# Extra bfloat16 products on TensorE ahead of the first expert, and one exponential moved on ScalarE

## Chip, core and metric

The kernel runs on one core of one Trainium2 chip. The metric is the device time of one execution in microseconds (us). The engines are PE (TensorE; PEld is its loading of weights), DVE (VectorE), ACT (ScalarE), POOL (GpSimd) and SP (SyncE, which only issues transfers).

## What is computed

Two halves share the input `x = A_q` (2048 tokens of 512 channels) and are mixed by a gate per token:

```
g = sigmoid((x * gate_w).sum(-1))
a = q * (causal_conv(shift_conv(k) * v, ssm_k) + D * ...)      # long convolution by FFT
b = sum over the top 2 of 8 experts: gate_e * (silu(x Wg) * (x Wu)) Wd
out = g * a + (1 - g) * b
```

The expert of a token is chosen by the two largest of its eight router logits `x @ w_router`. Each expert has 1376 hidden units. Everything is float32; the kernel splits the factors of its large products into a high and a low part of PE's faster 32-bit type and multiplies three times.

## The kernel before

One core does all of it. PE is the busy engine. The order of a run is this:

1. **Router.** SP loads the transposed input in 16 pieces `xt` (4 batches `c` of 4 pieces of 256 KB). For each batch PE multiplies the four pieces by the router weights, each into 32 partitions of one bank `lgp` (L509), ACT copies the bank to `lgT` (`keep`, L472), and PE turns it into `lg_ps` (`turn`, L488), nine columns for each of 16 token blocks; column 8 is the gate's logit. DVE copies the logits and ranks them (`ranks`, L493). `turn(c-1)` and `ranks(c-1)` are written between the two halves of batch `c`; those of the last batch come after the loop (L511).
2. **Counts and the first list.** DVE makes a mask and a running count (L518, L520), PE sums it over partitions into `cn_ps` (L526, L527), DVE works out the place of each token of the fullest expert and a table `hots` of ones and zeros (L535 to L618), PE turns the table into a list of token numbers (L624), DVE writes it as `gidx` (L600).
3. **First gather.** POOL fetches the listed rows by five indirect transfers (`load_rows`, L372); PE transposes each block of 128 rows (`turn_rows`, L381), ACT and DVE write its two parts `xh` and `xl` (L383, L384).
4. **Experts.** For each of 8 experts and 11 groups of hidden units PE does gate and up products `g` and `u` (`up`, L755, by `mm3`, L186), and down products (L804). The long convolution runs as filler between them (`tick`, L349).

Between the steps 1 to 3 stand pieces of the convolution's first stage on its kernel `ssm_k`: `plan(k)` (L461) issues `k_out` for the pieces named in `SEQ`: PE multiplies `kr` by `c` into two banks (`ks..p`, L239), ACT evicts each (L221) and issues its write to `kd` (L222). `plan(0)` issues piece `ks1`, `plan(2)` `ks2` and `ks3`, `plan(4)` `ks4` and `ks5`.

Up to L638 the order on all engines is the order in which the code is written (`tc.manual_schedule`, L432, closed at L638); after it a scheduler in the framework orders the instructions by its own timeline. PE, ACT, DVE and POOL each work through their queue in order. PSUM has eight banks; `lg_ps`, `lgp`, `cn_ps` and the experts' `g` and `u` share three of them (tag `gu`). `sums` (L439) is a bfloat16 tile whose parts 2 and 3 POOL fills with 1.0 and -1.0 at the very start (L440, L441).

The exponential of the gate's logits, `G` (L522), reads `lg_ps` on ACT; before the change it is written after `plan(0)`, so behind both evictions of `ks1`.

Of the kernel before, what the change touches and what calls it, by code (L numbers as in the profile page):

```python
# [14 lines left out]
AF = mybir.ActivationFunctionType  # L15
# [7 lines left out]
D = 512  # L23
KT = D // P
F = 1376
E = 8
PL = S // P
# [26 lines left out]
XG = 3  # L54
Z0, Z1 = (7, 6)
RM = 5
SEQ = "o0||o1 o2||o3 o4".split("|")
SEQ_N = max(int(w[1:]) for w in " ".join(SEQ).split() if w[0] == "o") + 1
VD = (1, 2, 3, 4, 5, 6)
# [70 lines left out]
def gated_mix(ctx: ExitStack, tc: tile.TileContext, a, out):  # L130
    nc = tc.nc
    sync, act, dve, pool, pe = nc.sync, nc.scalar, nc.vector, nc.gpsimd, nc.tensor
# [14 lines left out]
    G = cp.tile([P, PL], F32, name="G")  # L147
# [19 lines left out]
    def turned(name):  # L167
        return ps.tile([P, D], F32, tag="y", bufs=3, name=name)
# [84 lines left out]
    def k_load(pl):  # L253
        kr[pl] = load("B", BB, f"kr{pl}", rows(a["ssk"], pl), late=KL)
        if pl == 0:
            dD = t2k("T", 3, "dD")[0:1, :]
            sync.dma_start(dD, a["ssd"])
            pool.tensor_add(kr[0][0:1, :], kr[0][0:1, :], dD)

    def k_out(pl):  # L260
        stage1_f32(kr[pl], kd, pl, f"ks{pl}")
# [172 lines left out]
    lg_ps = ps.tile([P, D], F32, tag="gu", bufs=3, name="lg_ps")  # L434
# [4 lines left out]
    sums = rp.tile([P, 4, P], BF16, name="sums")  # L439
# [21 lines left out]
    def plan(k):  # L461
        for w in SEQ[k].split():
            i = int(w[1:])
            if w[0] == "l":
                k_load(k_order[i])
            else:
                k_out(k_order[i])
# [4 lines left out]
    def keep(c):  # L472
        lgT.append(rp.tile([P, D], F32, tag="lgT", bufs=4, name=f"lgT{c}"))
        act.activation(lgT[c], lgp[c], AF.Copy)
# [7 lines left out]
    lgv = lg_ps[:, :PL * 16].rearrange("p (a b) -> p a b", b=16)  # L482
# [5 lines left out]
    def turn(c):  # L488
        for pl in range(c * CP, c * CP + CP):
            pe.matmul(lg_ps[:, pl * 16:pl * 16 + E + 1], lgT[c][:, pl % CP * P:pl % CP * P + P], pick, start=True, stop=True)  # L490


    def ranks(c):  # L493
        part = slice(c * CP, c * CP + CP)
        dve.tensor_copy(L[:, part], lgv[:, part, :E])
        for x in range(E):
            for lo, hi, cmp in ((0, x, ALU.is_ge), (x + 1, E, ALU.is_gt)):
                if hi > lo:
                    dve.tensor_tensor(gt[:, part, lo:hi, x], L[:, part, x:x + 1].to_broadcast([P, CP, hi - lo]),
                                      L[:, part, lo:hi], op=cmp)  # L500
        dve.tensor_reduce(rank[:, part], gt[:, part], op=ALU.add, axis=AX.X)

    for c in range(NB):
        lgp.append(ps.tile([P, D], F32, tag="gu", bufs=3, name=f"lgp{c}"))
        for kt in range(KT):
            if c and kt == 2:
                turn(c - 1)
                ranks(c - 1)
            pe.matmul(lgp[c][32 * kt:32 * kt + 32], wk[:, kt], xts[c * KT + kt], start=True, stop=True)  # L509
        keep(c)  # L510
    turn(NB - 1)  # L511
    ranks(NB - 1)
    pool.tensor_copy(sums[:, 0], before)
    pool.tensor_add(before, before, ident)
# [4 lines left out]

    dve.tensor_tensor_scan(run[:, 1:].rearrange("p e a -> p (e a)"), ones, mask.rearrange("p e a -> p (e a)"),  # L520
                           0.0, op0=ALU.mult, op1=ALU.add)
    act.activation(G, lgv[:, :, E], AF.Exp, scale=-1.0)  # L522
    plan(1)
    cn_ps = ps.tile([P, D], F32, tag="gu", bufs=3, name="cn_ps")
    for o, (x, y) in ((0, (2, 3)), (16, (0, 1))):
        pe.matmul(cn_ps[:, o:o + E], sums[:, x], run[:, 1:, PL - 1], start=True, stop=False)  # L526
        pe.matmul(cn_ps[:, o:o + E], sums[:, y], run[:, :E, PL - 1], start=False, stop=True)  # L527
    plan(2)
    cnt = cn_ps[:, :E]
    key = rp.tile([P, E], F32, name="key")  # L530
    top = rp.tile([P, 1], F32, name="top")
# [60 lines left out]
    def read(k, pv):  # L592
        c0, n, f0, f1 = chunks[k]
        cs = slice(c0, c0 + n)
        m = min(MAIN, c0 + n)
        if f0 == 0:
            dve.tensor_scalar(idf[:, cs], pv[:, 0], dummy, None, op0=ALU.add)
            dve.tensor_add(idf[:, cs], idf[:, cs], pv[:, 1])
            if c0 < MAIN:
                i = dve.tensor_scalar(gidx[:, c0:m], idf[:, c0:m], float(S - 1), None, op0=ALU.min)  # L600
                anchor.setdefault("dve", i.ins)
                anchor.setdefault("dve k", i.ins)
        if f1 > 2:
            dve.scalar_tensor_tensor(wsum[:, cs], idf[:, cs], float(S), spare[:, cs], op0=ALU.is_ge, op1=ALU.mult)
            dve.tensor_add(sidx[:, cs], idf[:, cs], wsum[:, cs])
            dve.tensor_copy(wsum[:, cs], pv[:, 2 - f0])
            dve.tensor_add(wsum[:, cs], wsum[:, cs], pv[:, 3 - f0])
            dve.tensor_add(slot_w[:, cs], wsum[:, cs], pv[:, 4 - f0])
# [12 lines left out]
    list0 = ps.tile([P, D], F32, tag="y", bufs=3, name="list0")  # L621
    pv0 = list0[:, :2 * TILES].rearrange("p (f c) -> p f c", f=2)
    for i in range(PL):
        pe.matmul(pv0, hot[:, i], val0[:, i], start=(i == 0), stop=(i == PL - 1))  # L624
    read(0, pv0)
    l1, z, ll = mi2[:, 224:240], mi2[:, 240:256], te(mf2, PL * E)
# [6 lines left out]
    rows0 = gather(0)  # L633
    next(rows0)
    plan(4)
    for _ in range(RM):
        next(rows0, None)
    order.close()  # L638
    ordered = False
    for _ in rows0:  # L640
# [285 lines left out]
    with tc.For_i(0, nb_v, 1) as b:  # L926
        with tc.tile_pool(name="over", bufs=1) as op:
# [9 lines left out]
            p = turned("oxp").rearrange("p (k n) -> p k n", k=KT)  # L937
# [5 lines left out]
            for ft, (f0, fw) in enumerate(FT):  # L943
                n = 2 * KT * fw
# [66 lines left out]
```

## Time and profile before

| | us |
|---|---|
| three runs | 985.08, 985.34, 989.24; median 985.34 |
| the profiled execution | 989.02 |
| its span, first to last instruction | 987.2 |
| mean granted PE clock in it | 0.981 of full speed |
| PE busy | 956.7 (97%) |
| DVE, ACT, POOL busy | 658.1, 559.3, 163.2 |

Busy time is the sum of an engine's instruction times, overlaps counted once. The granted clock stands at one of two levels, 2.4 GHz (1.00) and 1.2 GHz (0.50). All times below count from the start of the span.

### The profile page before, as it was taken

The page shows a single profiled execution, that of the slowest core. Times are in us where ns is not written, and L with a number is a line of the kernel's source. Part 1 is how long each engine was busy: PE and PEld are TensorE (multiplying, and loading weights), DVE is VectorE, ACT ScalarE, POOL GpSimd, SP SyncE. Part 2 cuts the span into 40 slices and gives each one's busy share as a digit, 9 for nine tenths or more (in the row PEclk, how much of TensorE's full clock was granted, in tenths as well). Part 3 has the DMA queues.
Part 4 walks back from the last instruction along what each step waited for, and adds up shares of the span by engine and source line. Part 5 has one row for each costly group of instructions (what it writes and reads, how often), then busy time and mean ns, then how long its engine had stood idle before and what let it go on. Part 6 is the DMA issues. An engine that isn't in the chain of part 4 may idle for free. (4 is left out here: it accounts for less than half of the span.)

```text
span 987.2 us, 18708 instructions
## 1 busy us (share of the span) xinstructions
PE 956.7 (97%) x6944; PEld 876.0 (89%) x6944; DVE 658.1 (67%) x1318; ACT 559.3 (57%) x1066; POOL 163.2 (17%) x165
## 2 busy tenths in 40 slices
PE   7699999999999999999999999999999999999995
PEld 3388998999999999999999999999999999867893
DVE  3599569979999754756766576675776567554541
ACT  1464334554555643787677777688776777513330
POOL 0202010210203020131111312041113010023202
PEclk7699999999999999999999999999999999999998
DMA  7775694455656544576545646475557552699813
GB/s 253 266 263 192 238 312 153 151 169 180 213 191 181 179 134 167 152 181 185 160 140 161 167 150 198 147 171 157 180 154 190 158 175 84 206 305 273 213 31 43
DMA packets 88400, 178.24 MB, mean 181 GB/s; under 512 B 10513, under 2 KB 19601, under 8 KB 88178
## 3 DMA queue, kind: packets, MB, share of 16 engines
q1 hardware_dynamic: 54322, 119.40, 37.1%
q0 software_dynamic: 19296, 30.08, 15.3%
q10 hardware_dynamic: 14688, 27.53, 7.5%
q8 instruction: 56, 0.92, 0.4%
q14 instruction: 38, 0.31, 0.1%
HBM read 133.39 MB, written 43.57 MB: 179 GB/s over the span
## 5 line engine op out<-in xcount | busy, mean ns | idle before, releaser
L187 PE MATMUL g<-xh,gh 128*128 128x256 f32 (+13 forms) x704 | 203.7, 289 | 0.0
L187 PE MATMUL u<-xh,gh 128*128 128x256 f32 (+13 forms) x704 | 201.8, 287 | 1.7 <-ACT sg L786 1.6
L188 PE MATMUL u<-xl,gh 128*128 128x256 f32 (+13 forms) x704 | 201.1, 286 | 0.0
L189 PE MATMUL g<-xh,gl 128*128 128x256 f32 (+13 forms) x704 | 201.0, 286 | 0.0
L189 PE MATMUL u<-xh,gl 128*128 128x256 f32 (+13 forms) x704 | 200.9, 285 | 0.0
L188 PE MATMUL g<-xl,gh 128*128 128x256 f32 (+13 forms) x704 | 200.9, 285 | 0.0
L187 PEld LDWEIGHTS g<-xh,gh 128*128 128x128 f32 (+1 forms) x704 | 131.0, 186 | 14.9 <-issue 5.4
L187 PEld LDWEIGHTS u<-xh,gh 128*128 128x128 f32 (+1 forms) x704 | 131.1, 186 | 6.3 <-issue 2.3
L188 PEld LDWEIGHTS g<-xl,gh 128*128 128x128 f32 (+1 forms) x704 | 131.1, 186 | 3.8 <-issue 0.8
L189 PEld LDWEIGHTS u<-xh,gl 128*128 128x128 f32 (+1 forms) x704 | 131.0, 186 | 3.0 <-issue 1.6
L189 PEld LDWEIGHTS g<-xh,gl 128*128 128x128 f32 (+1 forms) x704 | 131.1, 186 | 2.5 <-issue 0.8
L188 PEld LDWEIGHTS u<-xl,gh 128*128 128x128 f32 (+1 forms) x704 | 131.1, 186 | 1.8
L788 ACT ACTIVATE hh<-sg 128x256 fp32r<-128x256 f32 (+13 forms) x176 | 73.7, 419 | 98.1 <-DVE sg L787 96.6
L187 PE MATMUL yp<-hh,dh 128*128 128x266 f32 (+10 forms) x440 | 127.4, 290 | 0.0
L188 PE MATMUL yp<-hl,dh 128*128 128x266 f32 (+10 forms) x440 | 126.8, 289 | 0.0
L189 PE MATMUL yp<-hh,dl 128*128 128x266 f32 (+10 forms) x440 | 126.6, 289 | 0.0
L787 DVE TENSOR_TENSOR sg<-sg,u 128x256 f32<-128x256 f32 (+13 forms) x176 | 74.8, 425 | 75.9 <-PE u L189 55.3
L771 DVE TENSOR_TENSOR gl<-raw,gh 128x1024 fp32r<-128x1024 f32 (+1 forms) x88 | 105.3, 1197 | 24.7 <-ACT gh L769 24.2
L786 ACT ACTIVATE sg<-g 128x256 f32<-128x256 f32 (+13 forms) x176 | 67.5, 386 | 80.0 <-PE g L189 73.2
L769 ACT ACTIVATE gh<-raw 128x1024 fp32r<-128x1024 f32 (+1 forms) x88 | 91.2, 1036 | 34.0 <-PE u L188 29.7
L789 DVE TENSOR_TENSOR hl<-sg,hh 128x256 fp32r<-128x256 f32 (+13 forms) x176 | 75.3, 428 | 32.7 <-ACT hh L788 32.2
L801 DVE TENSOR_TENSOR dl<-rd,dh 128x512 fp32r<-128x512 f32 (+1 forms) x88 | 59.5, 687 | 52.3 <-ACT dh L799 48.0
(1035 smaller groups left out, 1801.0 us busy)
## 6 DMA issues: line engine op xcount, KB each, us to landing
raw<-in_wgu SPq DMA_DIRECT2D x77, 512.0 KB
rd<-in_wd SPq DMA_DIRECT2D x77, 256.0 KB
kl<-kd SPq DMA_DIRECT2D x32, 256.0 KB
xl<-xd SPq DMA_DIRECT2D x32, 256.0 KB
zd<-ze ACTq DMA_DIRECT2D x32, 256.0 KB
zl<-zd SPq DMA_DIRECT2D x32, 256.0 KB
out<-zt SPq DMA_DIRECT2D x21, 256.0 KB
krow<-in_kpad SPq DMA_DIRECT2D x19, 256.0 KB
```

Of the source, the lines that this page charges most:

```text
L187: pe.matmul(p, wh, hi, start=start, stop=False)
L188: pe.matmul(p, wh, lo, start=False, stop=False)
L189: pe.matmul(p, wl, hi, start=False, stop=stop)
L769: act.activation(gh[:, :n], raw[:, :n], AF.Copy)
L771: dve.tensor_sub(gl[:, :n], raw[:, :n], gh[:, :n].bitcast(F32))
L786: act.activation(sg[:fw, :nn], pp[0][:fw, :nn], AF.Silu)
L787: dve.tensor_mul(sg[:fw, :nn], sg[:fw, :nn], pp[1][:fw, :nn])
L788: act.activation(hh[:fw, sl], sg[:fw, :nn], AF.Copy)
L789: dve.tensor_sub(hl[:fw, sl], sg[:fw, :nn], hh[:fw, sl].bitcast(F32))
L801: dve.tensor_sub(dl[:fw], rd[:fw], dh[:fw].bitcast(F32))
```

## The change

A helper `warm(n, p)` issues `n` products of a 128x128 tile of ones by a 128x256 tile of ones and minus ones, both bfloat16, into columns 256 to 511 of the bank `p`. Nobody reads these columns. `WARM` gives the counts: 14 before the router, 2 after each of the four products of batch 0 (8 in all), 6 before the last `turn`, 16 before the counts, 20 before the list, 6 in its middle, 26 before the first transposes, and 8 after each of the first four blocks of transposes (32): 128 products in all. The exponential `G` moves from behind `plan(0)` to just behind the last `turn`.

```diff
+WARM = (14, 2, 6, 16, 20, 6, 26, 8)
...
+    def warm(n, p):
+        for _ in range(n):
+            pe.matmul(p[:, D // 2:], sums[:, 2], sums[:, 2:].rearrange("p a b -> p (a b)"), start=True, stop=True)
+
+    warm(WARM[0], lg_ps)
     for c in range(NB):
...
             pe.matmul(lgp[c][32 * kt:32 * kt + 32], wk[:, kt], xts[c * KT + kt], start=True, stop=True)
+            if c == 0:
+                warm(WARM[1], lg_ps)
         keep(c)
+    warm(WARM[2], lg_ps)
     turn(NB - 1)
+    act.activation(G, lgv[:, :, E], AF.Exp, scale=-1.0)
     ranks(NB - 1)
...
-    act.activation(G, lgv[:, :, E], AF.Exp, scale=-1.0)
     plan(1)
+    warm(WARM[3], lg_ps)
     cn_ps = ps.tile([P, D], F32, tag="gu", bufs=3, name="cn_ps")
...
     plan(2)
+    warm(WARM[4], cn_ps)
...
     for i in range(PL):
+        if i == PL // 2:
+            warm(WARM[5], cn_ps)
         pe.matmul(pv0, hot[:, i], val0[:, i], start=(i == 0), stop=(i == PL - 1))
...
     plan(4)
-    for _ in range(RM):
+    warm(WARM[6], cn_ps)
+    for i in range(RM):
         next(rows0, None)
+        if i < RM - 1:
+            warm(WARM[7], cn_ps)
     order.close()
```

How the instructions stand now is shown at three places. The line numbers after the change are some 1 to 17 higher.

**DVE's copy of the last batch of logits**, with the semaphores that each instruction waits for. Before:

```order
L501 TENSOR_REDUCE r_160<-gt 128x32 [waits DVE_49]
L495 COPY r_160<-lg_ps 128x32 [waits PE_49]
L499 TENSOR_TENSOR gt<-r_160 128x4x7 [waits DVE_49]
```

After:

```order
L502 TENSOR_REDUCE r_160<-gt 128x32 [waits DVE_49]
L496 COPY r_160<-lg_ps 128x32 [waits Activation_49]
L500 TENSOR_TENSOR gt<-r_160 128x4x7 [waits DVE_49]
```

The copy waited for PE's `turn`; now it waits for ACT, that is for the exponential that reads the same bank.

**ACT from the exponential to the first weights' high part** (`gh`), `s` being a small tile of the routing. Before:

```order
L221 ACTIVATE ks1e_284<-ks1p_278 128x512
L222 DMA kd<-ks1e_284 128x512 [waits DMAHW7_49,Activation_49]
L522 ACTIVATE G<-lg_ps 128x16 [waits DVE_49]
L750 TENSOR_LOAD eor_78 [waits DVE_49]
L221 ACTIVATE ks2e_300<-ks2p_296 128x512 [waits PE_49]
L222 DMA kd<-ks2e_300 128x512 [waits DMAHW2_49,Activation_49]
L221 ACTIVATE ks2e_303<-ks2p_297 128x512
L769 ACTIVATE gh_0_469<-raw_0_467 128x1024 [waits DMAHW0_49]
L222 DMA kd<-ks2e_303 128x512 [waits DMAHW3_49,Activation_49]
L221 ACTIVATE ks3e_310<-ks3p_306 128x512 [waits DMAHW6_49,PE_49]
```

After:

```order
L222 ACTIVATE ks2e_347<-ks2p_341 128x512
L223 DMA kd<-ks2e_347 128x512 [waits DMAHW2_49,Activation_49]
L222 ACTIVATE ks3e_354<-ks3p_350 128x512 [waits DMAHW6_49,PE_49]
L223 DMA kd<-ks3e_354 128x512 [waits DMAHW3_49,Activation_49]
L222 ACTIVATE ks3e_357<-ks3p_351 128x512 [waits DMAHW7_49]
L223 DMA kd<-ks3e_357 128x512 [waits DMAHW4_49,Activation_49]
L767 TENSOR_LOAD eor_78 [waits DVE_49]
L786 ACTIVATE gh_0_597<-raw_0_595 128x1024 [waits DMAHW5_49]
L646 ACTIVATE s_165<-s_165 128x16 [waits DVE_49]
```

`gh` of the first weights, which waits for a transfer, stood ahead of one write of `ks2` and all of `ks3`; now it stands behind them. Further on, ACT's issues of `rd_0`, `raw_1` and `rd_1` (256, 512 and 256 KB of weights) move from behind `xh` of the third block to behind that of the first.

**PE from the third block of transposes to the first expert's products.** Before:

```order
L381 MATMUL xgp_2_423<-ident,xg_2_383 128x128 x3
L239 MATMUL ks6p_721<-kr_445,c_90 128x512 [waits DMAHW5_49,Activation_49]
L239 MATMUL ks6p_720<-kr_445,c_90 128x512 [waits Activation_49]
L187 MATMUL g_0_0_475<-xh_377,gh_0_469 128x256 [waits Activation_49]
L187 MATMUL u_0_0_488<-xh_377,gh_0_469 128x256
L381 MATMUL xgp_3_430<-ident,xg_3_385 128x128 [waits DMASW4_49,DVE_49]
```

After (each stretch of eight added products shown by its first pair of rows or its last):

```order
L382 MATMUL xgp_2_535<-ident,xg_2_453 128x128 x3
L507 LDWEIGHTS sums
L507 MATMUL cn_ps<-sums 128x256
...
L240 MATMUL ks6p_849<-kr_573,c_90 128x512 [waits DMAHW5_49,Activation_49]
L382 MATMUL xgp_3_550<-ident,xg_3_455 128x128 [waits DMASW4_49,DVE_49]
...
L188 MATMUL g_0_0_603<-xh_447,gh_0_597 128x256 [waits Activation_49]
L382 MATMUL xgp_4_565<-ident,xg_4_457 128x56 [waits DMASW5_49,DVE_49]
```

Eight added products stand behind the third block and eight behind the fourth; one of the two products of `ks6`, and the first `u` product, move behind the first `g` group.

## Rows read from the trace of the kernel before

**Rows 1.** The page: span, and the granted clock in 40 equal slices.
```profile
span 987.2 us, 18708 instructions
...
PEclk7699999999999999999999999999999999999998
```

**Rows 2.** Timeline of PE, 5 to 27 us: start, length, line, instruction, count, idle before.
```profile
5.08 5.36 PE L509 MATMUL lgp<-xt,wr 128*32 128x512 f32 x12 [5.08 <-DMA xt<-in_qT]
10.38 1.06 PE L490 MATMUL lg_ps<-wr,lgT 128*128 128x9 f32 x8
11.37 1.13 PE L509 MATMUL lgp<-xt,wr 128*32 128x512 f32 x8
13.14 1.56 PE L490 MATMUL lg_ps<-wr,lgT 128*128 128x9 f32 x8 [0.64 <-ACT lgT L474]
14.63 1.94 PE L509 MATMUL lgp<-xt,wr 128*32 128x512 f32 x8
...
19.09 1.92 PE L509 MATMUL lgp<-xt,wr 128*32 128x512 f32 x4
21.73 1.88 PE L490 MATMUL lg_ps<-wr,lgT 128*128 128x9 f32 x8 [0.72 <-ACT lgT L474]
23.54 2.08 PE L239 MATMUL ks1p<-kr,c 64*128 64x512 f32 x4
26.55 0.17 PE L526 MATMUL cn_ps<-run,sums 128*128 128x8 bf16 x1 [0.93 <-DVE run L520]
```

**Rows 3.** Windows of 1 us, PE: length, busy, granted clock, DMA share, GB/s.
```profile
13.00:14.00 1.00, 0.86 (x6) 0.76 1.06 389
...
30.00:31.00 1.00, 0.53 (x2) 0.71 0.70 61
...
34.00:35.00 1.00, 0.00 (x0) 0.50 1.04 399
```

**Rows 4.** Timeline of PE, 31 to 49 us.
```profile
31.25 0.36 PE L624 MATMUL list<-vals,hots 128*128 128x10 bf16 x8 [0.72 <-DVE hots L617]
32.39 0.36 PE L624 MATMUL list<-vals,hots 128*128 128x10 bf16 x8 [0.78 <-DVE hots L617]
...
38.95 1.09 PE L381 MATMUL xgp<-ident,xg 128*128 128x128 f32 x4 [0.59 <-DMA xg<-in_q,gidx]
...
44.08 1.09 PE L381 MATMUL xgp<-ident,xg 128*128 128x128 f32 x4 [1.69 <-DMA xg<-in_q,gidx]
...
47.68 0.98 PE L381 MATMUL xgp<-ident,xg 128*128 128x128 f32 x8
48.60 0.39 PE L188 MATMUL g<-xl,gh 128*128 128x256 f32 x1
48.82 0.27 PE L189 MATMUL g<-xh,gl 128*128 128x256 f32 x1
48.94 0.28 PE L187 MATMUL g<-xh,gh 128*128 128x256 f32 x1
```

**Rows 5.** Timeline of ACT, 27 to 37 us (ACTq: its queue issuing a transfer).
```profile
27.69 0.18 ACT L522 ACTIVATE G<-lg_ps 128x16 f32<-128x16 f32 x1 [0.40 <-DVE s L543]
...
33.70 1.06 ACT L769 ACTIVATE gh<-raw 128x1024 fp32r<-128x1024 f32 x1 [2.84 <-DMA raw<-in_wgu]
33.76 0.36 ACTq L222 DMA_DIRECT2D kd<-ks2e  x1
...
36.27 0.33 ACTq L222 DMA_DIRECT2D kd<-ks3e  x1
```

**Rows 6.** Timeline of POOL: the first indirect transfer of the gather.
```profile
33.68 1.05 POOL L372 DMA_INDIRECT xg<-in_q,gidx  x1 [16.39 <-DVE gidx L600]
```

**Rows 7.** Window of the gather: busy of each engine, granted clock, DMA share, GB/s.
```profile
33.00:46.00 13.00, 7.96 (x22) 3.65 (x20) 4.59 (x15) 6.31 (x11) 5.72 (x5) 0.54 0.93 330
```

**Rows 8.** Waits of PE from 48.6 to 980 us: total, times, longest.
```profile
PE yp L336 <- DMA zl<-zd: 2.3, 3, 1.7
PE u L187 <- ACT sg L786: 1.6, 1, 1.6
```

## The prediction

> **What bounds the kernel now.** I read the page first. The span is 987.2 us, and the row of the granted clock is full in every slice but the first two and the last [rows 1]. So only the head can gain from a faster clock: some 48 us, from the first load to the stretch where PE runs product after product (from 48.60, [rows 4]). Behind it PE is bound by its own work; its only waits there are 1.6 us for a silu and 2.3 us for three loads [rows 8]. What the head saves moves the end one for one, as long as the first weights come earlier too.
>
> Then I followed the head on PE's timeline with the clock beside it. The clock stands at 2.4 GHz until it falls between 13 and 14 us (mean 0.76), is back between 30 and 31 (0.71), and is gone again at 34 (0.50) [rows 3]; the transposes at 47.68 run fast again, eight in 0.98 us against four in 1.09 at 44.08 [rows 4]. What PE did before the fall is one `turn`, four router products side by side, a pause of 0.64 us and the start of the next `turn` [rows 2]. From 13.5 on this chain is PE, ACT, PE in turn, until `turn(3)` ends at 23.61. After it DVE sets the pace up to the list (PE waits 0.93 for the counts, 0.72 and 0.78 for `hots` [rows 2, 4]), and then the gather: PE waits for the landing of three blocks, up to 1.69 us.
>
> The sum is made against the profiled execution, 989.02. The median of the runs is 3.68 lower, 985.34, and the four times form two pairs, near 985.2 and near 989.1. That gap matters below.
>
> **The change, part by part.** The added products have 256 columns, as the first expert's have; those start 0.12 us apart at full clock (48.82 and 48.94, [rows 4]). At half clock I take twice that, 0.24.
>
> *Router batches 1 to 3.* At full clock `turn` takes 1.06, at half 1.88 (three times: at 13.14, cut by the fall, 1.56, then twice 1.88, of which one is shown); four router products take 1.13 against 1.94; the last two took 1.92, for which I also put 1.13 [rows 2]. If the clock held, the chain would be shorter by 0.50 + 0.81 + 0.82 + 0.79 + 0.82 = 3.7 us. No product is added inside this stretch, so this term lies between 0 and -3.7. I take -3.7: it is the gap between the two pairs of runs, so two of three unprofiled executions probably have it already, and the earlier start of PE's work should not lose it. This is inferred from times, not seen in a trace.
>
> *The 14 and the 8 in batch 0.* The 14 take 3.4 us at half clock and fit before the first piece lands (idle 5.08, [rows 2]): nothing. The 8 are full-width and stand between products that use 32 columns each and now run side by side: six products take 5.36 us, paced by landing. If nothing overlaps any more, four times (1.13 + 0.24), then 1.13 for the pair, end at 11.7 where 10.44 was: +1.2. With all of it at half clock, four times (1.94 + 0.48) and 1.94 end at 16.7: +6.3. If the loads pace it still: 0. I take +0.6, as the clock should be up early.
>
> *Six before `turn(3)`.* 0.72 against the wait of 0.72 [rows 2]: 0; at half clock 1.44: +0.7.
>
> *The exponential.* DVE's copy now waits for it. It takes 0.18 [rows 5] plus a handover: +0.2. A page of the Trainium skill, PSUM — Partial Sum Buffer, section PSUM bank collisions raise a hardware error, asks that PSUM be guarded by bank and quadrant, not by address, and so speaks against sharing a bank; by that rule each reader and writer of `lg_ps` and `cn_ps` is kept apart. The order shows just this new wait on ACT. The sum would be +0.2 by the rule and 0 without it; the added products themselves come when the readers of their bank are long done.
>
> *Sixteen before the counts.* DVE needs 2.94 us from `turn(3)` to the counts (23.61 to 26.55), now 3.14. At full clock `ks1` and the sixteen take 1.13 + 1.92 = 3.05: 0. At half clock 2.08 + 3.84 = 5.9: +2.8.
>
> *Twenty and six around the list.* From the counts to the list are 4.70 us (26.55 to 31.25); at full clock twice 1.13 and twenty make 4.7: 0. The six (0.72) fit the wait of 0.78. The clock had come back at 30.6 after PE had worked without a pause through `ks2` and `ks3`; now that unbroken stretch begins with `ks1` at 23.5, so I expect full speed here.
>
> *Twenty-six before the transposes.* From the end of the list (32.75) to the first block are 6.2 us; `ks4`, `ks5` and 26 products take 2 x 1.13 + 3.1 = 5.4: 0.
>
> *From the third block to the products.* Now 44.08 to 48.60, 4.52 us. After, at full clock: transposes 0.5, eight products 0.96, one product of `ks6` at most 1.13, transposes 0.5, eight more 0.96, then 0.12 and 0.45: 4.6. The other half of `ks6` (0.5) comes behind: +0.6. The faster clock is eaten by products that fill no wait.
>
> *The gather.* Its first transfer starts at 33.68 [rows 6]; from 33 to 46 the DMA engines are 0.93 busy at 330 GB/s [rows 7]. Three writes of 256 KB, issued from 33.76 to 36.27 because `gh` waits 2.84 us ahead of them [rows 5], now go before it. At 390 GB/s [rows 3] that clears 2.0 us. Against it 1.0 MB of weights is now issued behind the first block, not the third: up to +2.6 if all of it lands ahead of the last blocks. I take -1.4: the writes leave for certain, and of the weights I count the first 256 KB, 0.6.
>
> *Later waits* [rows 8] can vanish or grow, since the scheduler's order behind the head differs: -3.9 to +3.9, taken as 0.
>
> Sum: -3.7 + 0.6 + 0.2 + 0.6 - 1.4 = -3.7, so 989.0 - 3.7 = **985.3 us**: better than the profiled execution, and even with the median.
>
> **The rivals.** About 0.5% (4.9 us) is what a measurement of this kernel can tell from no change.
>
> *The clock falls again at 13.5* as the rows show, since batches 1 to 3 are as before, and comes back only among the sixteen. Then the change does not do what it says up to the counts: 0 for batches 1 to 3 and for batch 0, +0.7 for the six, +0.2, +0.9 for the sixteen (a third of 2.8, as the unbroken work begins there), +0.6, -1.4: +1.0, so 990.0, just within 0.5% of the median (990.3). The fall itself speaks for it, the two pairs of runs against it. I give it 0.26. A page of the Trainium skill, TensorE: Matmul & The Clock Gate, section Why this matters for your kernels, names long idle gaps between bursts of matmuls as what brings the clock down. By that rule the clock would have held here, and the term of -3.7 would be free before any change, so that the sum against this execution would be 0.0 and its time 989.0. The trace disagrees: PE's only pause in the stretch before the fall is 0.64 us. What chance that outcome keeps lies in the 0.26.
>
> *Slower.* Half clock when `ks1` begins, and still at the sixteenth product: the counts, and DVE's whole chain behind them, come late. +0.7 + 0.2 + 2.8 + 0.6 (batch 0) + 0.6 - 1.4 = +3.5: 992.5. It decides whether PE's stretch from 23.5 brings the clock back before the sixteen are through; the return at 30.6 speaks for that. 0.08.
>
> *Faster.* The clock holds, batch 0 costs nothing, the gather gains 2.0, its transposes and weights come early enough that the +0.6 is covered, and the later waits of 3.9 us go: -3.7 + 0.2 - 2.0 - 3.9 = -9.4: 979.6. With part of it, 980.4 is the bound for 0.5%. 0.13.
>
> **How the numbers follow.** The forecast case has 0.53, so within 0.5%: 0.53 + 0.26 = 0.79; faster 0.13; slower 0.08. The likeliest case alone runs from 982 (gather -2.0, silu wait gone) to 988.4 (half of batch 0 at half clock, +3.7 in place of +0.6). The range takes in the fall at 13.5 and the weaker half of the faster case: 980.5 to 990.0.
>
> **What would show it.** Right: full clock from the router's second batch to the list, `turn(3)` ending near 20.2, the counts waiting for DVE and not for the added products, products without a break from about 45. Wrong: a clock of 0.50 around 17 to 25, `turn` still at 1.88, the counts directly behind the last added product, or the first blocks of the gather landing later than 6.1 us after the list.

## The result and the profile after

The changed kernel takes **996.81 us** (median of 6 runs, 993.68 to 998.43) where the kernel before took 985.54 beside it (6 runs, 982.5 to 989.24): ratio 1.0101, 95% interval 1.0079 to 1.0122. It is slower by 11 us, 6.8 above the range's upper end. Measured again (`f1_change`, 6 runs), it took 997.81 (ratio 1.0112 [1.0078, 1.0145]).

The profiled executions are 989.02 before and 997.70 after: 8.68 to explain, 8.67 of it inside the span. The page of after, against [rows 1]:

```profile
span 995.9 us, 18969 instructions
...
PE 972.0 (98%) x7072; PEld 887.0 (89%) x7072; DVE 658.7 (66%) x1318; ACT 560.8 (56%) x1066; POOL 159.5 (16%) x165
...
PEclk7899999999999999999999999999999999999998
```

PE has 128 instructions more, as the change says, and is busy for 15.3 us more. The row of the clock is a little fuller. It says nothing of where the time went; the timeline of PE does (columns as in [rows 2]):

```profile
10.89 1.06 PE L491 MATMUL lg_ps<-wr,lgT 128*128 128x9 f32 x8
...
13.66 1.17 PE L491 MATMUL lg_ps<-wr,lgT 128*128 128x9 f32 x8 [0.71 <-ACT lgT L475]
14.76 1.94 PE L516 MATMUL lgp<-xt,wr 128*32 128x512 f32 x8
17.40 1.88 PE L491 MATMUL lg_ps<-wr,lgT 128*128 128x9 f32 x8 [0.71 <-ACT lgT L475]
19.21 1.92 PE L516 MATMUL lgp<-xt,wr 128*32 128x512 f32 x4
21.07 1.46 PE L507 MATMUL lg_ps<-sums 128*128 128x256 bf16 x6
22.32 1.72 PE L491 MATMUL lg_ps<-wr,lgT 128*128 128x9 f32 x8
...
25.98 2.94 PE L507 MATMUL lg_ps<-sums 128*128 128x256 bf16 x16
28.76 0.18 PE L537 MATMUL cn_ps<-run,sums 128*128 128x8 bf16 x1
...
30.86 2.36 PE L507 MATMUL cn_ps<-sums 128*128 128x256 bf16 x20
37.65 0.36 PE L638 MATMUL list<-vals,hots 128*128 128x10 bf16 x8 [4.43 <-DVE hots L629]
...
53.92 0.39 PE L189 MATMUL g<-xl,gh 128*128 128x256 f32 x1
```

Up to the end of `turn(3)` little differs: 22.32 + 1.72 = 24.04, against 21.73 + 1.88 = 23.61 [rows 2]. Then two steps open. The counts come 1.8 us later behind it, directly behind the sixteen, most of which ran at half clock (the clock is back at 28.1). And between the counts and the list, where before has 4.70 us (26.55 to 31.25), lie 8.89; PE waits 4.43 of them for `hots`. Why DVE is late shows on its own timeline, first before, then after:

```profile
26.85 0.17 DVE L535 SCALAR_TENSOR_TENSOR key<-cn_ps,rc 128x8 f32<-128x8 f32 x1 [0.44 <-PE cn_ps L527]
```

```profile
24.29 0.19 DVE L496 COPY r<-lg_ps 128x32 f32<-128x32 f32 x1 [2.98 <-ACT G L522]
...
26.62 0.42 DVE L531 TENSOR_TENSOR_SCAN run<-ones,mask 128x128 bf16<-128x128 f32 x1
33.26 0.17 DVE L547 SCALAR_TENSOR_TENSOR key<-cn_ps,rc 128x8 f32<-128x8 f32 x1 [6.21 <-PE cn_ps L507]
```

`key` is DVE's first read of the counts. Before, it starts 0.30 us behind the start of the counts' first product, released by L527, the counts. After, it starts 4.50 behind, released by **L507**, the added products: the last of the twenty ends at 30.86 + 2.36 = 33.22. The read and all that DVE does behind it up to `hots` start 4.2 us later in the chain.

The rest of the path, from the list on: POOL's first indirect transfer follows the list as before (2.46 us against 2.43 behind its start), and the unbroken products start 13.8 us behind that transfer, where before had 14.9. From their start to PE's last end are 930.0 us against 926.7.

The rows of POOL and of ACT that answer to [rows 5, 6]:

```profile
40.11 1.05 POOL L373 DMA_INDIRECT xg<-in_q,gidx  x1 [22.93 <-DVE gidx L612]
```

```profile
24.07 0.18 ACT L522 ACTIVATE G<-lg_ps 128x16 f32<-128x16 f32 x1 [2.27 <-PE lg_ps L491]
...
39.89 1.06 ACT L786 ACTIVATE gh<-raw 128x1024 fp32r<-128x1024 f32 x1 [6.12 <-DMA raw<-in_wgu]
```

| step | before | after | difference |
|---|---|---|---|
| start to `turn(0)` | 10.38 | 10.89 | +0.5 |
| `turn(0)` to the end of `turn(3)` | 13.23 | 13.15 | -0.1 |
| to the counts | 2.94 | 4.72 | +1.8 |
| counts to `key` | 0.30 | 4.50 | **+4.2** |
| `key` to the list | 4.40 | 4.39 | 0.0 |
| list to the first transfer | 2.43 | 2.46 | 0.0 |
| to unbroken products | 14.92 | 13.81 | -1.1 |
| to PE's last end | 926.74 | 930.02 | +3.3 |
| to the end of the span | 11.88 | 11.95 | +0.1 |

The +3.3 has three parts. Three pairs of the convolution's products that stood side by side are pulled apart, and the one pair that was apart before stands together. Such a pair (`ks8p`, each product on half of PE's rows) starts 1.05 us ahead of what follows it when together, first row, before; apart, two rows, after, each product costs as much alone:

```profile
57.48 1.13 PE L239 MATMUL ks8p<-kr,c 64*128 64x512 f32 x4
58.53 0.38 PE L187 MATMUL u<-xh,gh 128*128 128x256 f32 x1
```

```profile
69.80 1.12 PE L240 MATMUL ks8p<-kr,c 64*128 64x512 f32 x2
70.86 0.39 PE L188 MATMUL g<-xh,gh 128*128 128x256 f32 x1
...
77.33 1.12 PE L240 MATMUL ks8p<-kr,c 64*128 64x512 f32 x2
78.39 0.39 PE L188 MATMUL g<-xh,gh 128*128 128x256 f32 x1
```

Summed from start to start, `ks6`, `ks8` and `ks11` are +1.05 each and `ks9` is -1.04: +2.1. PE's late waits shrank by 1.0, from 3.9 us [rows 8] to some 2.9. The other 2.2 is spread over gate, up and down products and late transposes; its cause is not shown. The late waits after:

```profile
PE yp L337 <- DMA zl<-zd: 1.1, 2, 0.8
PE u L188 <- ACT sg L803: 0.8, 2, 0.6
PE yt L877 <- DVE ya L845: 0.7, 1, 0.7
PE g L190 <- DVE gl L788: 0.2, 1, 0.2
```

### The profile page after: what moved, and what is told of

It reads as the page before. It is cut to its first block, busy times and chain, and to the rows that moved or that the text cites. A ratio compares the mean times of both kernels' runs of the same rounds, so it can differ in the third digit from the quotient of the medians.

```text
span 995.9 us, 18969 instructions
## 1 busy us (share of the span) xinstructions
PE 972.0 (98%) x7072; PEld 887.0 (89%) x7072; DVE 658.7 (66%) x1318; ACT 560.8 (56%) x1066; POOL 159.5 (16%) x165
## 5 line engine op out<-in xcount | busy, mean ns | idle before, releaser
L816 ACT ACTIVATE dh<-rd 128x512 fp32r<-128x512 f32 (+1 forms) x88 | 53.4, 628 | 72.5 <-DMA rd<-in_wd 32.0
```

What stands on the lines that cost most here:

```text
L816: act.activation(dh[:fw], rd[:fw], AF.Copy)
```

## The experiments

Each was run in five rounds beside the kernel before; ratios are to that one, with 95% intervals. Single executions of one kernel lie up to 10 us apart (`f2_twenty` below: 986.6 to 996.6); in the profiled ones alone `turn(3)` ends between 18.67 and 24.04 us, by when the clock falls in the router and by the products added there. So the time of a kernel is its median, and a profile shows one execution's mechanism. The loss can lie in three places: the twenty (**theory A**: DVE's first read of the counts waits for them), the tail (the six, the twenty-six and the eights) and the router. For the first runs rival B is that the twenty only fill a wait.

### The twenty behind the reads, or left out; the router alone; no products

`e1_behind` writes the twenty behind DVE's second read of the counts:

```diff
     plan(2)
-    warm(WARM[4], cn_ps)
...
     dve.tensor_add(posE, run[:, 1:], cn_ps[:, 16:16 + E].unsqueeze(2).to_broadcast([P, E, PL]))
+    warm(WARM[4], cn_ps)
```

> The twenty products stand behind DVE's two reads of the counts in cn_ps instead of ahead of them. Theory A (those reads wait for the last of the twenty, since the wait is kept by bank): the first read starts 0.3 us after the counts' last product instead of 4.4, so 4.1 us less; only one pair of ssm_k products (ks12) is pulled apart by the scheduler instead of three (ks6, ks8, ks11), worth 1.05 us each by the traces, so 2.1 less: about 990.5 against 996.8, ratio to before 1.005. Rival B (half clock and the products ahead of the counts are the cause, not the wait): only the 2.1 go, 994.7, ratio 1.009.

`e2_no20` leaves them out:

```diff
-WARM = (14, 2, 6, 16, 20, 6, 26, 8)
+WARM = (14, 2, 6, 16, 0, 6, 26, 8)
```

> The change without the twenty; the same three ssm_k pairs are apart, so nothing but the wait (and the clock behind it) differs from the changed kernel. Theory A: DVE's read 0.3 us behind the counts, 4.1 us less than 996.8: 992.7, ratio 1.007. Rival B: no change, 996.8, ratio 1.011; a third reading, that the twenty are needed to hold the clock for the list and the gather, would give more than 996.8.

`e5_router_only` keeps only those up to the counts:

```diff
-WARM = (14, 2, 6, 16, 20, 6, 26, 8)
+WARM = (14, 2, 6, 16, 0, 0, 0, 0)
```

> The products up to the counts (14, 8, 6, 16) stay, the twenty and all behind go; one pair apart (ks9). Theory A: the cost left is that of the products ahead of the counts, 2.2 us in the profile of the changed kernel: 987.8, ratio 1.002. Rival B (these carry most of the loss): ratio over 1.006.

`e3_g_only` keeps none, so that only the exponential is moved:

```diff
-WARM = (14, 2, 6, 16, 20, 6, 26, 8)
+WARM = (0, 0, 0, 0, 0, 0, 0, 0)
```

> Leaves out all added products; only the exponential stands ahead of the evictions. One pair apart (ks9), as before. Theory A: DVE's copy of the last logits starts some 0.4 us after PE's last turn instead of 0.04, and nothing else: 985.9, ratio 1.000. Rival: the exponential and the wait on ACT cost much of the 11 us: ratio over 1.003.

| kernel | us, median (lowest to highest, runs) | ratio |
|---|---|---|
| `e1_behind` | 991.04 (987.40 to 995.09, 11) | 1.0050 [1.0031, 1.0069] |
| `e2_no20` | 992.58 (988.01 to 997.28, 7) | 1.0074 [1.0047, 1.0101] |
| `e5_router_only` | 987.29 (985.01 to 991.21, 12) | 1.0007 [0.9986, 1.0028] |
| `e3_g_only` | 985.77 (982.86 to 989.26, 12) | 0.9996 [0.9977, 1.0014] |

All four come out as theory A says. In `e1_behind` DVE's read is released by the counts again, 0.30 us behind their start (first PE, then DVE):

```profile
27.71 0.18 PE L537 MATMUL cn_ps<-run,sums 128*128 128x8 bf16 x1
```

```profile
28.01 0.17 DVE L546 SCALAR_TENSOR_TENSOR key<-cn_ps,rc 128x8 f32<-128x8 f32 x1 [1.57 <-PE cn_ps L538]
```

The moved exponential costs nothing, the router's products nothing that can be told from zero. In `e1_behind` half of the loss goes; 0.5% is left, and by `e5_router_only` it lies behind the counts. But there two pairs fewer are apart as well. `e2_no20` has the same three pairs apart as the changed kernel, and by the ratios it is 2.7 us faster (by the medians, each against its own kernel before, 4.7).

### The twenty alone, and the tail alone

`e6_twenty_only`:

```diff
-WARM = (14, 2, 6, 16, 20, 6, 26, 8)
+WARM = (0, 0, 0, 0, 20, 0, 0, 0)
```

> Of all added products only the twenty stay, in the place where the change puts them, ahead of DVE's first reads of the counts; the gate's exponential stays early. Theory A (DVE's read of the counts waits for the last of the twenty, 4.1 us in the profile): against a kernel before at 985.9, 989.9 to 990.7 us (ratio 1.004 to 1.005), and in the profile 4 us or more from the start of the counts to DVE's first read, where the kernel before has 0.3. Rival B (the twenty only fill a wait; the loss of the change lies elsewhere): 985.5 to 987.0, ratio under 1.001.

`e7_tail_only`:

```diff
-WARM = (14, 2, 6, 16, 20, 6, 26, 8)
+WARM = (0, 0, 0, 0, 0, 6, 26, 8)
```

> Only the six in the list, the twenty-six behind it and the four eights stay; none up to the counts. Theory A (behind the twenty, what is left of the loss lies here: the third and fourth eights fill no wait, and three pairs of half-height products of the shared expert are pulled apart): with the runs so far, 991.0 without the twenty's wait less 1.3 for the router's products gives 989.7, and up to 991.8 with the pairs, 2.1; ratio 1.004 to 1.006. Rival C (the tail's products lie in waits, and only the pairs cost): 988.0, ratio 1.002. Rival D (the tail gains the clock and costs nothing): 984 to 986.

`e8_tail_fours`:

```diff
-WARM = (14, 2, 6, 16, 20, 6, 26, 8)
+WARM = (0, 0, 0, 0, 0, 6, 26, 4)
```

> As the kernel with the tail alone, but four products behind each block where eight were; the framework then leaves only one pair of half-height products apart, as in the kernel before. Theory A: half of the eights' cost and none of the pairs', 987.0 to 988.0, at least 2.5 us under the kernel with the eights. Rival C (only the pairs cost): 985.9, and 2.1 under it. Rival E (the loss is not from the eights nor the pairs, but from the twenty-six ahead of the blocks): within 1 us of the kernel with the eights.

`e6_twenty_only`: 990.48 (986.97 to 994.46, 12 runs), ratio 1.0044 [1.0024, 1.0064]. The twenty cost this much with nothing else added. PE and DVE in its profile, where the clock stood at half from 21 to 27 us:

```profile
21.83 0.17 PE L537 MATMUL cn_ps<-run,sums 128*128 128x8 bf16 x1 [2.10 <-DVE run L531]
...
25.73 3.02 PE L507 MATMUL cn_ps<-sums 128*128 128x256 bf16 x20
```

```profile
28.78 0.17 DVE L547 SCALAR_TENSOR_TENSOR key<-cn_ps,rc 128x8 f32<-128x8 f32 x1 [7.10 <-DMA kd<-ks3e]
```

The row names a transfer as the releaser, but the twenty end at 28.75, 0.03 us ahead of the read. The read is 6.95 us behind the start of the counts: in these two profiles the wait costs 4.2 us at full clock (the changed kernel) and 6.65 mostly at half.

`e7_tail_only`: 990.91 (988.23 to 994.25, 12), ratio 1.0040 [1.0022, 1.0058]. The tail costs as much as the twenty; rivals C and D, 988.0 at most, lie below its interval. `e8_tail_fours`: 988.44 (984.79 to 993.46, 12), ratio 1.0011 [0.9989, 1.0033]: 2.5 us under it. Fewer products and fewer pairs apart were changed at once here, so the next three try to part them.

### Pairs apart, and the third and fourth eights

Two kernels differ by nine products, but in one no pair of half-height products is apart, in the other three are. `e9_none_apart`:

```diff
-WARM = (14, 2, 6, 16, 20, 6, 26, 8)
+WARM = (0, 0, 0, 0, 0, 1, 1, 2)
```

> Ten added products in all: one in the list, one behind it, two behind each of four blocks; with these numbers the framework leaves no pair of half-height products apart (the kernel before has one). Theory C (a pair apart costs 1.05 us): 986.3 less 1.05, so 985.2 us, and 3.15 under the kernel with three pairs apart. Rival F (what a pair takes apart is taken out of waits elsewhere): the two within 1 us of each other.

`e10_three_apart`:

```diff
-WARM = (14, 2, 6, 16, 20, 6, 26, 8)
+WARM = (0, 0, 0, 0, 0, 0, 1, 0)
```

> One added product in all, behind the list; with it the framework leaves three pairs of half-height products apart. Theory C: 986.3 plus two more pairs, 2.1, so 988.4 us. Rival F: 986.3.

`e11_two_blocks` keeps the tail, with eights behind the first two blocks only:

```diff
-WARM = (14, 2, 6, 16, 20, 6, 26, 8)
+WARM = (0, 0, 0, 0, 0, 6, 26, 8)
...
-        if i < RM - 1:
+        if i < 2:
             warm(WARM[7], cn_ps)
```

> The kernel with the tail alone (six, twenty-six, eights), its eights behind the first two blocks only; one pair apart, as before. Theory A (the eights behind the third and fourth block, 2 x 0.96, and the two pairs, 2.1, are the tail's cost): 987.0 us, 4 under the kernel with all four eights. Rival C (pairs alone): 988.8, 2.1 under it. Rival E (the twenty-six delay the first block where the clock is half): 990 or more, within 1 us of it.

`e9_none_apart`: 985.52 (983.77 to 991.85, 12), ratio 0.9986 [0.9966, 1.0006]. `e10_three_apart`: 988.16 (984.43 to 992.23, 12), ratio 1.0019 [1.0000, 1.0038]. The three pairs cost 2.6 us by the medians and 3.3 by the ratios; 3.15 was expected. The intervals still touch, so the times weaken rival F and don't refute it.

`e11_two_blocks`: 986.91 (984.26 to 992.10, 12), ratio 1.0006 [0.9986, 1.0025]: under the tail with all four eights by 4.0 us by the medians and 3.4 by the ratios, near theory A's 4. The interval also holds rival C's 988.8; what speaks against C is the trace. PE from the third block on, in `e7_tail_only`:

```profile
40.16 0.60 PE L382 MATMUL xgp<-ident,xg 128*128 128x128 f32 x4
40.59 1.04 PE L507 MATMUL cn_ps<-sums 128*128 128x256 bf16 x8
41.56 1.12 PE L240 MATMUL ks6p<-kr,c 64*128 64x512 f32 x2
42.61 0.66 PE L382 MATMUL xgp<-ident,xg 128*128 128x128 f32 x4
43.10 1.04 PE L507 MATMUL cn_ps<-sums 128*128 128x256 bf16 x8
43.90 0.36 PE L188 MATMUL g<-xh,gh 128*128 128x256 f32 x1
```

and in `e11_two_blocks`:

```profile
41.78 0.60 PE L382 MATMUL xgp<-ident,xg 128*128 128x128 f32 x4
42.31 1.13 PE L240 MATMUL ks6p<-kr,c 64*128 64x512 f32 x4
43.38 0.66 PE L382 MATMUL xgp<-ident,xg 128*128 128x128 f32 x4
43.79 0.36 PE L188 MATMUL g<-xh,gh 128*128 128x256 f32 x1
```

From the third block to the first gate product are 3.74 us with the eights, 2.01 without: PE waits for nothing in either, the eights are delay (1.73 us), and the pair of `ks6` is parted. The profile of `e11_two_blocks` also shows the clock at half until 38.6 while the twenty-six take 5.18 us, and the median is that of before: rival E falls.

```profile
34.15 5.18 PE L507 MATMUL cn_ps<-sums 128*128 128x256 bf16 x26
```

### The mends together

`e12_mended` is the whole change with both mends: the twenty behind the reads, as in `e1_behind`, and `if i < 2`, as in `e11_two_blocks`. `v1_best` has both too, other numbers, and five products ahead of each `turn` of batches 1 to 3:

```diff
-WARM = (14, 2, 6, 16, 20, 6, 26, 8)
+WARM = (14, 0, 5, 14, 18, 6, 26, 8)
...
+                warm(5 if c > 1 else 0, lg_ps)
                 turn(c - 1)
```

> The whole change with two mends: the twenty behind DVE's reads of the counts, and the eights behind the first two blocks only; one pair apart, as before. Theory A: 996.8 less 4.1 (the twenty's wait), 2.1 (pairs) and 1.9 (eights), so 988.7 us, ratio 1.002 to 1.003, what is left being the router's products, 1.3. Rival E: 991, as with the twenty moved alone.

> A version put together from the parts that cost nothing: the twenty behind DVE's reads and eighteen in number, five products ahead of each turn of the router's batches 1 to 3, none in batch 0 behind the first fourteen, fourteen before the counts, eights behind the first two blocks only; one pair apart as before. If a held clock in the router's batches is worth the 3.7 us of the prediction and nothing new waits: 982 to 984 us, ratio 0.996 to 0.998. If the tail's twenty-six and eights still cost what the runs so far leave for them: 987 to 989.

`e12_mended`: 984.14 (982.13 to 989.72, 12), ratio 0.9983 [0.9962, 1.0003]. `v1_best`: 985.08 (982.80 to 989.17, 12), ratio 0.9983 [0.9966, 1.0001]. Both lost all of the 11 us, and more than theory A's 8.1 came back in `e12_mended`. So the change, each mend alone and both together ran on one chip (`f1_change` is the changed kernel, `f2_twenty` as `e1_behind`, `f3_eights` with `if i < 2` alone, `f4_both` as `e12_mended`):

> The changed kernel itself, beside its mended forms on one chip. 996 to 997.5 us, ratio 1.009 to 1.012, as measured before.

> The first mend alone, the twenty behind DVE's reads of the counts. Theory A (prices add): 4.1 to 5.8 under the changed kernel, 991 to 992.5 us.

> The second mend alone, eights behind the first two blocks only; the twenty stay ahead of DVE's read, one pair is apart. Theory A (prices add): 4.0 under the changed kernel, 992.5 us. Rival G (the two mends need each other: the eights cost only where the first products wait for nothing else): within 1.5 us of the changed kernel.

> Both mends. Theory A: the sum of the two, 8.1 under the changed kernel, 988.5 us. Rival G: more than the sum, 984 us, 12 to 13 under it, as one measurement had it; then the two prices measured apart are too small.

| | eights behind four blocks | behind two |
|---|---|---|
| twenty ahead of the read | `f1_change` 997.81, 1.0112 [1.0078, 1.0145] | `f3_eights` 997.41, 1.0097 [1.0064, 1.0130] |
| twenty behind it | `f2_twenty` 990.78, 1.0038 [1.0013, 1.0062] | `f4_both` 986.48, 1.0006 [0.9982, 1.0031] |

By the ratios the twenty cost 7.3 us without and 9.0 with the other mend, the eights 1.5 and 3.2. The pairs go along in part: in the traces three are apart in `f1_change`, one in each of the other three, so 7.3 and 1.5 contain two pairs, 9.0 and 3.2 none. Why the 9.0 is above the 4.5 us from the counts to the read in the trace of `f3_eights` is not shown. Theory A and rival G can't be parted: the intervals of `f1_change` and `f3_eights` are 0.7% wide, and hold both 0 and 4 us between the two. What `e12_mended` gave above the sum did not come again (`f4_both` is 2.3 us slower than it was); the two intervals overlap, so it may have been spread.

### The same place, another bank

```diff
     plan(2)
-    warm(WARM[4], cn_ps)
+    warm(WARM[4], lg_ps)
```

That is `g1_bank`; `g2_bank_blocks` has `if i < 2` besides.

> The changed kernel with one word different: the twenty keep their place in PE's order, ahead of DVE's reads of the counts, but write into lg_ps's bank, not into cn_ps's, which holds the counts. Theory A (DVE's read waits because they share the tile that it reads): the read comes about 0.3 us behind the counts' start and the time is that of the twenty behind the reads, 990.8 us, ratio 1.004. Rival H (it is the place in PE's order, or the twenty's load on PE, whatever bank they write): 4 us or more from the counts to the read, 997 us.

> The same, with the eights behind the first two blocks only. Theory A: as the kernel with both mends, 984 to 986.5 us, ratio 0.998 to 1.001. Rival H: as the kernel with the second mend alone, 997.4 us.

`g1_bank`: 989.74 (986.09 to 993.41, 7), ratio 1.0048 [1.0025, 1.0071]. `g2_bank_blocks`: 985.09 (983.42 to 990.25, 12), ratio 1.0008 [0.9991, 1.0025]. Both are the times of the twenty behind the reads, with the twenty where the change put them. PE and DVE in `g1_bank`:

```profile
23.07 0.18 PE L537 MATMUL cn_ps<-run,sums 128*128 128x8 bf16 x1 [0.16 <-DVE run L531]
...
25.19 2.36 PE L507 MATMUL lg_ps<-sums 128*128 128x256 bf16 x20
27.77 0.36 PE L638 MATMUL list<-vals,hots 128*128 128x10 bf16 x8 [0.22 <-DVE hots L629]
```

```profile
23.38 0.17 DVE L547 SCALAR_TENSOR_TENSOR key<-cn_ps,rc 128x8 f32<-128x8 f32 x1 [0.37 <-PE cn_ps L538]
```

DVE reads 0.31 us behind the start of the counts, while `ks2`, `ks3` and the twenty run, and PE waits 0.22 for the list. So the wait comes from writing into the tile, and with it the bank, that DVE reads; place and load are not its cause. Rival H falls. Tile and bank are one here, so which of the two counts is not shown. Of the time of `g1_bank`, two pairs fewer apart than in the changed kernel are a part; `f3_eights` and `g2_bank_blocks` both have one apart, and differ by 8.8 us by the ratios.

## Why the prediction was wrong

**The step that failed: "Twenty and six around the list".** It was put at 0, since two pieces of the convolution and twenty products fit into the 4.70 us from the counts to the list. That counted PE's time, not DVE's wait. The twenty write columns of `cn_ps` that nobody reads, but DVE's first read of the counts stands behind them in the program, in the same tile, and waits for the last of them. So the 4.4 us of DVE's chain do not run beside `ks2`, `ks3` and the twenty but behind them: +4.2 in the profile, 4.3 us of time alone (`e6_twenty_only`). In the changed kernel the ratios give 2.7 (`e2_no20`), 5 to 7 where two pairs fewer are apart as well (`e1_behind`, `f2_twenty`, `g1_bank`), and 9 with the second mend (`f3_eights` against `f4_both` and `g2_bank_blocks`): the wait is shown, its price only to this range. None of the rivals had it.

Against the profile of before the sum was -3.7 and the measured difference is +8.7, so 12.4 us are to be accounted for: 4.2 are this wait, 3.6 the router's batches with the six, 3.3 PE's work behind the head, 1.6 the sixteen with the exponential, and the rest makes -0.3. The router's term counts only against that profile: with the median the forecast of 985.3 was even. Of the loss against the median, measured alone and by the ratios, the twenty are 4.3 us, the tail 3.9 (`e7_tail_only`), the products up to the counts 0.7.

The prediction quoted a page of the Trainium skill, PSUM — Partial Sum Buffer, section PSUM bank collisions raise a hardware error, and then said that the added products "come when the readers of their bank are long done". By that page's rule, guard by bank and quadrant and not by address, the free half of the bank is no protection. The trace agrees: 4.50 us from the counts to the read with the shared bank, 0.31 with another. The section adds that the compiler's back end makes two engines' instructions on one bank and quadrant wait for each other; who set the wait here, no run shows. For the sixteen, the six and the router's products the sentence held; for the twenty it was not looked at who reads `cn_ps` next.

The other steps:

- *"From the third block to the products", +0.6*: against the profile of before the stretch came out nearly as summed, 4.44 us (49.48 to 53.92) where 4.6 was forecast and before had 4.52: the clock gave what the eights took. The other half of `ks6` was put at 0.5 and costs 1.05. Against a kernel that has the clock without them, the eights are undersized: from the third block to the first gate product are 3.74 us in `e7_tail_only`, 2.01 in `e11_two_blocks`, so 1.7 of delay.
- *"Later waits", 0*: in the profile of after the waits indeed did not grow (in others they do: 8.4 us behind the head in `g1_bank`, 7.2 in `e1_behind`, against 3.9), but the term left out work: the pairs pulled apart cost +2.1 in the profile. That the order behind the head would differ was said; that PE's work there can itself get longer was not.
- *"Router batches 1 to 3", -3.7, inferred from the two pairs of runs*: in the profile of after the clock falls at 14.5 all the same, and `turn` and the four products are back at 1.88 and 1.92. Without the six the stretch shrank by 0.6, since the fall came 1 us later. As to the median the runs support the inference. Of the eight profiles with no product in the router, `turn(3)` ends between 18.67 and 19.46 in five (`e3_g_only`, `e6_twenty_only`, `e7_tail_only`, `e10_three_apart`, `e11_two_blocks`), at 20.98 in `e8_tail_fours`, and at 23.25 and 23.61 in `e9_none_apart` and before. So executions without these products often hold the clock that far already. With them the clock holds to 28 us or later in 6 of 12 profiles, without them in none of 8; but where it holds and batch 0 has its eight, `turn(3)` ends at 19.86 to 20.89, later than in those five.
- *Sixteen before the counts, 0 (bound +2.8)*: +1.8, because the half clock lasted to 28.1. This is the "Slower" rival's mechanism; it explains the lesser part, and in the median little, where all products up to the counts cost 0.7 us ([-1.4, +2.8], `e5_router_only`). Three of the four signs that were to show the forecast wrong are in the rows above (half clock from 17 on, `turn` at 1.88, the counts directly behind the sixteen); none of them pointed at DVE's read.
- *Batch 0, +0.6*: +0.5 in this pair of profiles, by luck: the profile of before has the latest `turn(0)` of the nine without these eight (9.31 to 10.38, median 9.64), and the eleven with them start it at 10.21 to 11.54, median 10.91, so +1.3, near the bound for no overlap (+1.2). *The six, 0 (bound +0.7)*: at half clock, `turn(3)` starts 1.19 us behind the end of the batch's last products (19.21 + 1.92) where before had 0.72, so +0.5. *The exponential, +0.2*: DVE's copy starts 0.25 us behind the end of `turn(3)`, where before had 0.04, here hidden by the sixteen; alone (`e3_g_only`) the ratio is 0.9996.
- *The gather, -1.4*: with the +0.6 of the blocks it gave -1.1 where -0.8 was the sum; the clock differs in this stretch too (0.54 before [rows 7], 1.00 after from 41.8 on), so the parts are not told apart. `gh` of the first weights, which ACT writes at 39.89 behind a wait of 6.12, is 13 us ahead of the products.

The clock, on which the prediction turned most, does not explain the loss: the changed kernel's mean granted clock is 0.987 to 0.995 in its six runs, that of the kernel before 0.976 to 0.986 in the 140 beside the experiments, and yet the change is slower. Four windows of after (length; busy time of PE, PEld, DVE, ACT and POOL; then clock, DMA share and GB/s as in [rows 3]):

```profile
14.00:15.00 1.00, 1.00 (x11) 0.93 (x14) 0.14 (x1) 0.00 (x0) 0.00 (x0) 0.73 1.08 341
...
28.00:29.00 1.00, 1.00 (x14) 0.84 (x12) 0.00 (x0) 0.00 (x0) 0.00 (x0) 0.95 0.91 350
...
38.00:39.00 1.00, 1.00 (x15) 0.58 (x12) 0.73 (x1) 0.00 (x0) 0.00 (x0) 0.67 0.94 379
...
41.00:42.00 1.00, 1.00 (x6) 0.31 (x2) 1.00 (x1) 0.00 (x0) 0.70 (x2) 0.62 0.26 33
```

It falls at 14.5, is back at 28.1, falls again at 38.3, behind the 4.43 us in which PE waits for `hots`, and is back at 41.8. In `e1_behind`, `e12_mended`, `f4_both`, `g1_bank` and `g2_bank_blocks`, which don't have that wait, it doesn't fall between 28 and 49 us (in `g1_bank` it does at 49.1); in `e2_no20`, `f2_twenty` and `v1_best`, which don't have it either, it falls at 29.1, 37.9 and 36.2. So the wait is not the only thing that brings it down.

## What to carry to other kernels

Filler work is free only if nothing in another queue waits for it: for each added instruction, look up who next touches its tile or its PSUM bank, at whatever columns, and put the filler behind that reader or in a bank that has none. Where a scheduler orders what follows, compare the cost of the work behind the edit too, since pairs that ran side by side may come apart. And where executions differ by several us, one profile tells the mechanism, the medians of many runs the price.

## What had not been expected

- A head at full clock throughout is worth almost nothing in the median. In `g2_bank_blocks` the window from 4 to 41 us reads 1.00 throughout, and the unbroken products start at 40.85, 7.75 us ahead of the profile of before:

```profile
4.00:41.00 37.00, 33.99 (x231) 18.96 (x230) 19.09 (x103) 11.38 (x20) 6.73 (x8) 1.00 0.91 309
```

  Its profiled execution is 983.55, 5.5 us under that of before (2.2 were given back behind the head: 929.0 us to PE's last end against 926.7), yet the ratio to before is 1.0008. Much of the gain is in the usual executions already: `e3_g_only`, with no added product, starts the unbroken products at 43.46 in a profile of 985.18. `f4_both` and `g2_bank_blocks` show every sign that was to prove the forecast right (`turn(3)` ends at 20.11 and 19.86, the counts wait for DVE, unbroken products from 43.21 and 40.85), and no gain in the median.
- Within a kernel the time goes with the clock granted to the execution. Of the 140 executions of the kernel before, 41 have a mean clock of 0.980 or less (median 988.4 us) and 52 have 0.985 or more (984.5). Of the 36 of `e12_mended`, `f4_both` and `g2_bank_blocks`, 12 have 0.991 or less (989.8) and 19 have 0.995 or more (983.9). So the mended change has a higher clock, but its better executions end where the better ones of before end. That is read from times and clocks side by side; no run sets the clock by itself.
- One added product behind the list (`e10_three_apart`) changes how the framework orders PE's work behind it, with 2.6 to 3.3 us between that kernel and one with ten.
- No version beats the kernel before beyond doubt; the two best read 0.9983, with intervals that end at 1.0001 and 1.0003, and `f4_both`, the same kernel as `e12_mended`, read 1.0006 the second time.
